# Seven quarter products for eight: Strassen's algorithm in the first half of an FFN behind attention

## The chip, the core and the metric

The kernel runs on one core of a Trainium2 chip. The metric is the device time of one execution in microseconds (us), the median of several runs. Beside it stands one execution recorded by the hardware profiler, with every instruction's start and length. The engines are TensorE (PE, matrix products; its weight loads are listed as PEld), VectorE (DVE), ScalarE (ACT), GpSimd (POOL) and SyncE (SP), which here issues all DMAs.

## The reference

Attention with normalized queries and keys, and then an FFN with two linear branches that are multiplied:

```python
# q, k, v: (8, 12, 448, 64); g_q, g_k: (64,)
q_n, k_n = rmsnorm(q, g_q), rmsnorm(k, g_k)       # x / sqrt(mean(x*x) + 1e-6) * g
attn = softmax(q_n @ k_n.T / 8)
x = (attn @ v).transpose(0, 2, 1, 3).reshape(3584, 768)
a, b = x @ w_a, x @ w_b                           # (768, 1536) each
out = (a * b) @ w_out                             # (1536, 768)
```

The weights arrive as float64; the kernel reads them as pairs of 32-bit words and rounds them to float32 itself. All products are in float32, and each float32 matmul is two instructions on TensorE.

## The kernel before

**Attention** is done by pairs of heads: 8 batches x 6 pairs are 48 pairs p. SP loads q, k and v; the squares are summed, POOL raises the means to the power -0.5 (L315), DVE scales q (L319), TensorE transposes k and q (L336), and ACT or DVE copy them into `qkT`. For each quarter c of the keys, TensorE makes the scores of both heads (L362), ACT the exponentials into `ET` (L368), and TensorE multiplies v by them into `o` (L381). The softmax's divisors come from `sums_over_keys`: a product with ones (L411) and a reciprocal on DVE (L415). For the first 12 pairs (`LEAD`) TensorE sums all four quarters of the keys; later DVE and POOL add them up first (L393, L395). `put_out` copies `o` (L460) and multiplies it by the reciprocal (L465) into `xT`, the transposed input of the FFN. A pair is written into its batch's block of tokens; blocks are cut at multiples of 128 tokens, so they hold 384 and 512 in turn, and what is over goes through `tail` into the next.

**The FFN** (`ffn(b)`, one block): for each of 12 column groups m and each of the weights a and b, 6 matmuls of 128 rows add up a bank `pf` (L491); ACT copies the bank of a into `hT` (L500) and DVE multiplies it by the bank of b (L502). Then for each 128 tokens and each half of the output 12 matmuls make `po` (L515); DVE or ACT copy it (L524, L526) and SP stores it. `pf` and `po` share two PSUM banks (tag `mm`); `hT` has one buffer, `xT` two.

**The weights** are made in 72 units of 384 columns (`weights(n)`): a DMA, one step on ACT (L250), five on DVE (L251 to L258), one on POOL (L260). The units of w_a and w_b, 48, come first, and use w_out's place for their raw words; then come w_out's 24.

**The order** is written by a planner, `Plan`. Every operation has an engine, an estimated length, a key, and the names that it reads and writes. The planner runs all of them in a model of the engines: each time it takes, on the engine that can start first, the ready operation with the lowest key (on TensorE among those that can start within 0.2 us of the first). Operations with the same `chain` stay together. The result is a fixed order for each engine's queue, which then runs in that order. The keys of attention are pair numbers, up to 48; those of the FFN start at 10,000. So TensorE does attention when some is ready, and FFN otherwise:

```python
op("PE", len(cs) * N / 600, key, products, ...)        # key = 1e4 + b * 1e3
op("PE", 0.76, p, product, ..., mode="rows", chain=chain)
```

## Time and profile before

| | |
|---|---|
| Median of 3 runs | 1820.95 us (1819.86 to 1821.93) |
| The profiled execution | 1819.57 us |
| Its span, first to last instruction | 1817.8 us |
| Mean granted TensorE clock | 0.991 |
| ACT busy | 384.3 us (21%) |
| POOL busy | 457.3 us (25%) |
| DMA | 73.43 MB, 40 GB/s over the span |

The page gives, for each engine, the busy time in us, its share of the span and the number of instructions. A line of a group names the source line, the engine, the operation, output<-input, the shape and the count; then come busy time, the mean of one in ns, the idle time of the engine just before these instructions, and what ended that. A line of the timeline gives the start, the length and what ran (merged with its like, xcount), and in brackets the idle time before it with what ended it. L numbers are lines of the kernel above. Lengths of matmuls include the filling and draining of the array, so consecutive ones overlap in the record; pitches from start to start do not.

### The profile page before, as it was taken

What the parts mean: (1) busy time and instruction counts of PE and PEld (TensorE: products, weight loads), DVE (VectorE), ACT (ScalarE), POOL (GpSimd) and SP (SyncE); (2) the same over time, 40 slices, a digit from 0 to 9 for tenths busy, and PEclk for the clock granted to TensorE, in tenths of its full rate; (3) what the DMA queues carried; (4) which work ended last, traced back from release to release, by engine and by line L of the source; (5) the groups of instructions that cost most, each with busy time, mean ns of one, the idle gap of its engine ahead of it and who ended that gap; (6) DMA issues with size and microseconds to landing.
All of it is one profiled execution on the core that took longest, in us unless ns stands there. A gap on an engine that the chain in (4) does not pass through costs nothing. (4 is left out here: it accounts for less than half of the span.)

```text
span 1817.8 us, 15323 instructions
## 1 busy us (share of the span) xinstructions
PE 1761.7 (97%) x5904; PEld 860.4 (47%) x5904; DVE 640.5 (35%) x872; ACT 384.3 (21%) x738; POOL 457.3 (25%) x276
## 2 busy tenths in 40 slices
PE   5899889999999999999999999999999999999998
PEld 2334444444444455544444455544444455554455
DVE  7999998640023410443004420245002420000000
ACT  5655323321013210232002320123101310000000
POOL 4444455550014420344004440145102210000000
PEclk8999999999999999999999999999999999999999
DMA  7444223110001100111001110011000100000000
GB/s 234 142 133 124 65 76 104 52 54 6 0 15 49 49 16 0 39 49 31 0 0 44 44 39 1 20 44 50 5 0 20 32 14 0 5 22 0 0 9 28
DMA packets 87317, 73.43 MB, mean 40 GB/s; under 512 B 49348, under 2 KB 78020, under 8 KB 87236
## 3 DMA queue, kind: packets, MB, share of 16 engines
q1 hardware_dynamic: 87236, 72.38, 14.1%
q8 instruction: 48, 0.79, 0.2%
q14 instruction: 33, 0.27, 0.1%
HBM read 61.34 MB, written 11.01 MB: 40 GB/s over the span
## 5 line engine op out<-in xcount | busy, mean ns | idle before, releaser
L491 PE MATMUL pf<-xT,w_b_sb 128*128 128x512 f32 (+1 forms) x1152 | 453.7, 543 | 9.8 <-DVE hT L502 9.8
L515 PE MATMUL po<-w_out_sb,hT 128*128 128x384 f32 x1344 | 453.1, 490 | 0.0
L491 PE MATMUL pf<-xT,w_a_sb 128*128 128x512 f32 (+1 forms) x1152 | 452.4, 541 | 0.0
L515 PEld LDWEIGHTS po<-w_out_sb,hT 128*128 128x128 f32 x1344 | 249.2, 190 | 193.2 <-issue 35.9
L491 PEld LDWEIGHTS pf<-xT,w_b_sb 128*128 128x128 f32 x1152 | 217.7, 191 | 229.2 <-issue 144.3
L491 PEld LDWEIGHTS pf<-xT,w_a_sb 128*128 128x128 f32 x1152 | 216.9, 190 | 215.8 <-issue 143.1
L502 DVE TENSOR_TENSOR hT<-hT,pf 128x384 f32<-128x384 f32 (+1 forms) x96 | 59.5, 620 | 700.3 <-PE pf L491 700.3
L368 ACT ACTIVATE ET<-sc,ms 112x448 f32<-112x448 f32 x384 | 212.4, 635 | 228.4 <-PE sc L362 227.3
L395 POOL TENSOR_TENSOR sum<-sum,ET 112x896 f32<-112x896 f32 x72 | 153.2, 2128 | 426.3 <-DVE sum L393 280.2
L415 DVE RECIPROCAL su<-su 128x448 f32<-128x448 f32 x48 | 142.3, 2964 | 147.3 <-PE su L411 147.3
L500 ACT COPY hT<-pf 128x384 f32<-128x384 f32 (+1 forms) x96 | 51.0, 532 | 662.3 <-PE pf L491 662.3
L381 PE MATMUL o<-ET,v_sb 112*64 112x448 f32 x768 | 175.1, 561 | 4.1 <-ACT ET L368 3.9
L362 PE MATMUL sc<-qkT 64*112 64x448 f32 x768 | 172.2, 568 | 4.9 <-DVE qkT L348 3.6
L315 POOL TENSOR_TENSOR ms<-ms,expo 112x16 f32<-112x16 f32 x48 | 141.8, 2953 | 26.7 <-DVE ms L311 25.1
L362 PEld LDWEIGHTS sc<-qkT 64*112 64x112 f32 x768 | 61.7, 174 | 111.6 <-issue 93.5
L381 PEld LDWEIGHTS o<-ET,v_sb 112*64 112x64 f32 x768 | 53.1, 138 | 104.5 <-issue 81.6
L302 DVE TENSOR_REDUCE ms<-sq 112x8 f32<-112x512 f32 x96 | 65.5, 682 | 84.1 <-POOL sq L296 76.8
L443 POOL COPY xT<-tail 128x384 f32<-128x384 f32 x4 | 2.0, 504 | 326.3 <-PE pf L491 323.1
L319 DVE TENSOR_TENSOR qn<-q_sb,ms 112x512 f32<-112x512 f32 x48 | 61.9, 1290 | 59.2 <-PE pt L336 47.3
L524 DVE COPY o_sb<-po 128x384 f32<-128x384 f32 x28 | 15.6, 557 | 144.6 <-PE po L515 144.6
L296 POOL TENSOR_TENSOR sq<-k_sb 112x512 f32<-112x512 f32 x36 | 38.0, 1056 | 71.5 <-DMA k_sb<-in_k_dram 70.2
L460 ACT COPY xT<-o 128x384 f32<-128x384 f32 (+1 forms) x48 | 24.2, 505 | 145.8 <-PE o L381 123.9
(54 smaller groups left out, 748.8 us busy)
## 6 DMA issues: line engine op xcount, KB each, us to landing
q_sb<-in_q_dram SPq DMA_DIRECT2D x48, 224.0 KB, 2.9
k_sb<-in_k_dram SPq DMA_DIRECT2D x96, 112.0 KB, 2.9
v_sb<-in_v_dram SPq DMA_DIRECT2D x48, 224.0 KB, 2.6
w_out_sb<-in_moe_w_a_dram SPq DMA_DIRECT2D x24, 384.0 KB, 3.8
w_out_sb<-in_moe_w_b_dram SPq DMA_DIRECT2D x24, 384.0 KB, 4.3
raw<-in_moe_w_out_dram SPq DMA_DIRECT2D x24, 384.0 KB, 3.1
out_dram<-o_sb SPq DMA_DIRECT2D x16, 168.0 KB, 2.1
out_dram<-o_sb SPq DMA_DIRECT2D x16, 144.0 KB, 2.0
```

Of the source, the lines that this page charges most:

```text
L302: nc.vector.tensor_reduce(rs[p][:, "qk".index(nm)], xs["sq", nm, p], AX, ALU.add)
L315: nc.gpsimd.tensor_tensor(msf, msf, expo, ALU.pow)
L319: nc.vector.tensor_tensor(qns[p].rearrange("p j h d -> p h j d"), xs["q", p].rearrange("p h (j d) -> p h j d", d=D), rs[p][:, 0].rearrange ...
L362: nc.tensor.matmul(t[:, e, 0:S], lhsT=qkTs[p][rows, 1, c * SP:(c + 1) * SP], rhs=qkTs[p][rows, 0, :], start=True, stop=True)
L368: nc.scalar.activation(E[:, e], scs[p, c][:, e, 0:S], AF.Exp, scale=rs[p][:, 1, 2 * c + e:2 * c + e + 1])
L381: nc.tensor.matmul(os_[p][e * D:(e + 1) * D, :], lhsT=xs["v", p][:, e, c * D:(c + 1) * D], rhs=ETs[p, c][:, e], start=(c == 0), stop=(c == ...
L395: nc.gpsimd.tensor_tensor(sums[p][0:SP], sums[p][0:SP], ETs[p, c], ALU.add)
L415: nc.vector.reciprocal(sus[p], sus[p])
L491: nc.tensor.matmul(pfs[m, n][:, 0:N], lhsT=w_sb[:, c, m * P:(m + 1) * P], rhs=xTs[b][:, c, 0:N], start=(c == 0), stop=(c == KA - 1))
L500: nc.scalar.copy(x, y)
L502: nc.vector.tensor_tensor(x, x, y, ALU.mult)
L515: nc.tensor.matmul(held["po"][:, 0:HALF], lhsT=hTs[0][:, m, t * P:(t + 1) * P], rhs=w_out_sb[:, m, h * HALF:(h + 1) * HALF], start=(m == 0 ...
```

## The change

The products x @ w_a and x @ w_b are made by Strassen's algorithm, one level deep (the variant with shared sums). An input block is two batches, 896 tokens: its quadrants are the two halves of the features (384 each) by the two batches (448 tokens each). There are four such blocks, beta = 0 to 3. The weights' quadrants are halves of the features by halves of the columns (768). Eight products of quarters become seven, of 3 matmuls of 448 columns each, with sums made beforehand and afterwards:

- *Inputs.* `put_out` writes quadrants `x{batch}.{half}` from a ring of 9 tiles. Four chained subtractions on DVE (`combine`, 1344 columns each) make T3, the new B12, T2 and T4. Every product of the block waits for T3 and T4. The blocks of 384 and 512 tokens and their tails are gone.
- *Weights.* For each of 12 rounds n = (m, ab), `factors(n)` loads four quadrants' pieces as float64 words in two parts (four DMAs, 1.57 MB), rounds them in steps of 768 columns, and makes three further factors with three DVE operations and one on POOL. The seven factors of a round, 1.376 MB, lie in a ring of three tiles (`st`); `keep` stores them in DRAM. Block 0 uses them as they are made; for blocks 1 to 3, `stream` loads them again (36 loads). Raw words of the first three rounds lie in `hT`'s place, those of the others in the last four rows of w_out's.
- *w_out.* Its 12 rows are rounded one at a time, 768 columns a step; rows 0 to 7 through a slot in `hT`'s place, rows 8 to 11 through `st` tiles once all the factors have begun.
- *Products.* A round runs a(B11), b(T2), a(B21), d(B12), g(T3), d(B22), g(T4); a, b, d and g are banks from the same ring of two as before. ACT, DVE and POOL put together the four quarters of a or of a*b from them in `hT`.
- *Attention.* In the first 12 pairs the transposes go through the `mm` banks, half a pair ahead, `qkT` has two buffers, the sums over the keys come in two parts of two quarters, and ACT copies them out of PSUM before the reciprocal. The reciprocal is made in two halves everywhere. Scores stand ahead of the previous pair's values in the chains.
- *Planner.* It models rings of tiles itself: an operation that opens a tile can't start before the tile's predecessor in the ring has had its last user. Its DMA rate goes from 200 to 250 bytes per ns.

The output products are as before, now over 7 tiles of 128 tokens a block. The core of the diff:

```diff
+            t, count = 0.0, {}
+            for x in members(n):
+                for name in ops[x][8]:
+                    tag, bufs = self.tags[name]
+                    had = opened.setdefault(tag, [])
+                    k = len(had) + count.get(tag, 0) - bufs
+                    count[tag] = count.get(tag, 0) + 1
+                    if k >= len(had):
+                        return None
+                    if k >= 0:
+                        if left[had[k]]:
+                            return None
+                        t = max(t, last[had[k]])
+            return t
...
-                    dma = max(dma, t) + ops[x][7] / 200.0
+                    dma = max(dma, t) + ops[x][7] / 250.0
...
+            for e, n, emit, r, wr in round_steps(get):
+                rate = {"ACT": 950, "DVE": 1900 if n == 1 else 950, "POOL": 420}[e]
+                op(e, 0.17 + size / rate, key, emit, [{"x": x, "w": w}[c] for c in r], [{"x": x, "w": w}[c] for c in wr])
...
+        def factors(n):
+            m, ab = order[n]
+            src = (moe_w_a, moe_w_b)[ab]
+            key = n * 1.1 + 0.5
+            st = tile_of(f"st{n}", "st", 3)
+            def begin():
+                sts[n] = ld.tile([P, 7, KH * P], FP32, tag="st", name="st", bufs=3)
+            op(None, 0.0, key, begin, [], [f"{st}/{x}" for x in range(7)] + ["streaming", "begun"], new=[st])
+            for part, quarters in enumerate((((0, 0), (0, 1)), ((1, 1), (1, 0)))):
+                if n < FIRST:
+                    at = 2 * n + part
+                    rows = [f"{hraw}/{at}"]
+                    words = lambda at=at: hold["h"][:, at * NW:(at + 1) * NW]
+                else:
+                    at = KO - 4 + 2 * part
+                    rows = [f"out{at}", f"out{at + 1}"]
+                    words = lambda at=at: w_out_sb[:, at:at + 2].rearrange("p a b -> p (a b)").bitcast(U32)
+                def load(words=words, quarters=quarters):
+                    for x, (i, j) in enumerate(quarters):
+                        nc.sync.dma_start(
+                            words()[:, 768 * x:768 * (x + 1)].rearrange("p (k n) -> p k n", k=KH),
+                            src[j * KH * P:(j + 1) * KH * P, 2 * (i * HM + m * P):2 * (i * HM + (m + 1) * P)].rearrange(
+                                "(k p) n -> p k n", p=P))
+                op("SP", 1.0, key - 2.5, load, [], rows, kb=768)
+                rounding(key, NW // 2, lambda words=words, part=part: (
+                    words().rearrange("p (n w) -> p n w", w=2), sts[n][:, 2 * part:2 * part + 2].rearrange("p a b -> p (a b)")),
+                    rows[0], f"{st}/{2 * part}")
+            parts = [0, 0, 2, 2, 4, 5, 6]
+            for e, us, to, x, y, alu in (("DVE", 0.6, 4, 3, 2, ALU.add), ("POOL", 1.05, 5, 0, 3, ALU.subtract),
+                                         ("DVE", 0.6, 3, 4, 0, ALU.subtract), ("DVE", 0.6, 6, 1, 3, ALU.subtract)):
+                op(e, us, key, lambda e=e, to=to, x=x, y=y, alu=alu: (nc.vector if e == "DVE" else nc.gpsimd).tensor_tensor(
+                    sts[n][:, to], sts[n][:, x], sts[n][:, y], alu),
+                   [f"{st}/{parts[x]}", f"{st}/{parts[y]}"], [f"{st}/{parts[to]}"])
...
+            def keep():
+                kept[n] = dram.tile([P, 7 * KH * P], FP32, name=f"kept{n}")
+                nc.sync.dma_start(kept[n], sts[n].rearrange("p a b -> p (a b)"))
+            op("SP", 0.5, key, keep, [f"{st}/{x}" for x in range(7)], [f"kept{n}"], kb=1376)
...
+        def stream(beta, n):
+            st = tile_of(f"st{beta}.{n}", "st", 3)
+            def load():
+                t = sts[beta, n] = ld.tile([P, 7, KH * P], FP32, tag="st", name="st", bufs=3)
+                nc.sync.dma_start(t.rearrange("p a b -> p (a b)"), kept[n])
+            op("SP", 0.5, 10.0 * beta + n / 2, load, [f"kept{n}"] + ([f"wl{kc}" for kc in range(KO)] if (beta, n) == (1, 0) else []), [f"{st}/{x}" for x in range(7)] + ["streaming"], new=[st], kb=1376)
...
+        def round_out(kc):
+            key, name = 11.5 + kc / 12, f"out{kc}"
+            raws = {}
+            if kc < WE:
+                st = f"{hraw}/{SLOTS - 1}"
             else:
-                st, name = f"out.{n % KO}", f"{'a' if dst is w_a_sb else 'b'}.{c}.{kc}"
+                st = tile_of(f"stout{kc}", "st", 3)
...
+                def move():
+                    x = wk.tile([P, 2, S], FP32, tag="sum", name="sum")[:, 0]
+                    nc.scalar.copy(x, sus[p])
+                    sus[p] = x
+                op("ACT", 0.55, p - 0.5, move, [su], [t, "moved"], new=[t])
+                su = t
+            for x in range(2):
+                half = slice(x * S // 2, (x + 1) * S // 2)
+                op("DVE", 1.55, p, lambda half=half: nc.vector.reciprocal(sus[p][:, half], sus[p][:, half]), [], [su])
...
+        def ffn(beta):
+            b = 2 * beta
+            B11, B21, B12, B22 = quad(b, 0), quad(b, 1), quad(b + 1, 0), quad(b + 1, 1)
+            key = 1e4 + beta * 1e3
...
+                op("DVE", 1.7, -0.5, emit, [x, y], [to], new=[to] if first else [])
+            T2, T3, T4 = (f"T{beta}.{n}" for n in (2, 3, 4))
+            combine(T3, B22, B12, True)
+            combine(B12, B12, B11, False)
+            combine(T2, B22, B12, True)
+            combine(T4, B21, T2, True)
...
+            for n, (m, ab) in enumerate(order):
+                if beta:
+                    stream(beta, n)
+                    st, at = f"st{beta}.{n}", (beta, n)
+                else:
+                    st, at = f"st{n}", n
+                quarter_products(beta, key, m, ab, st, at, (B11, B21, B12, B22, T2, T3, T4), h)
+            seven = 2 * S // P
+            for t in range(seven):
...
+            def product(bank, f, x, start, stop):
+                nm = f"p{ident_}.{bank}"
+                if start:
+                    tile_of(nm, "mm", 2)
...
+                def emit():
+                    if start:
+                        banks[bank] = ps_mm.tile([P, 512], FP32, tag="mm", name="pq")
+                    for c in range(KH):
+                        nc.tensor.matmul(banks[bank][:, 0:S], lhsT=sts[at][:, f, c * P:(c + 1) * P], rhs=quads[x][:, c],
+                                         start=(start and c == 0), stop=(stop and c == KH - 1),
+                                         skip_group_check=True)
+                op("PE", KH * S / 600, key, emit, [f"{st}/{(0, 0, 2, 2, 4, 5, 6)[f]}", x, T3, T4], [nm, "ffn"], new=[nm] if start else [], mode="full")
+                return nm
...
+            a = product("a", 0, B11, True, False)
+            if ab == 0:
+                take("ACT", 0.55, lambda: nc.scalar.copy(C(0, 0), PS("a")), [a], [hp[0]])
+            else:
+                t1 = tile("t1")
+                take("ACT", 0.55, lambda: nc.scalar.copy(fresh("t1", "t", 2), PS("a")), [a], [t1], [t1])
+            b_ = product("b", 3, T2, True, True)
+            if ab == 0:
+                take("DVE", 0.68, lambda: V.tensor_tensor(fresh("U", "U", 1), C(0, 0), PS("b"), ALU.add), [b_, hp[0]], [U], [U])
+            else:
+                take("DVE", 0.68, lambda: V.tensor_tensor(fresh("U", "U", 1), held["t1"], PS("b"), ALU.add), [b_, t1], [U], [U])
+            product("a", 1, B21, False, True)
+            if ab == 0:
+                take("ACT", 0.55, lambda: nc.scalar.copy(C(0, 0), PS("a")), [a], [hp[0]])
+            else:
+                take("DVE", 0.68, lambda: V.tensor_tensor(C(0, 0), C(0, 0), PS("a"), ALU.mult), [a], [hp[0]])
+            d = product("d", 4, B12, True, False)
+            if ab == 0:
+                take("DVE", 0.68, lambda: V.tensor_tensor(C(1, 1), held["U"], PS("d"), ALU.add), [d, U], [hp[1]])
+            else:
+                t2 = tile("t2")
+                take("DVE", 0.68, lambda: V.tensor_tensor(fresh("t2", "t", 2), held["U"], PS("d"), ALU.add), [d, U], [t2], [t2])
+            g = product("g", 5, T3, True, False)
+            if ab == 0:
+                take("DVE", 0.68, lambda: V.tensor_tensor(C(1, 1), C(1, 1), PS("g"), ALU.add), [g], [hp[1]])
+            else:
+                take("DVE", 0.68, lambda: V.tensor_tensor(held["t2"], held["t2"], PS("g"), ALU.add), [g], [t2])
+                take("POOL", 1.15, lambda: nc.gpsimd.tensor_tensor(C(1, 1), C(1, 1), held["t2"], ALU.mult), [t2], [hp[1]])
+            product("d", 6, B22, False, True)
+            product("g", 2, T4, False, True)
+            for bank, nm, i, n in (("d", "t3", 0, 1), ("g", "t4", 1, 0)):
+                if ab == 0:
+                    take("DVE", 0.68, lambda bank=bank, i=i, n=n: V.tensor_tensor(C(i, n), held["U"], PS(bank), ALU.add),
+                         [f"p{ident_}.{bank}", U], [hp[i]])
+                else:
+                    t = tile(nm)
+                    take("DVE", 0.68, lambda bank=bank, nm=nm: V.tensor_tensor(fresh(nm, "t", 2), held["U"], PS(bank), ALU.add),
+                         [f"p{ident_}.{bank}", U], [t], [t])
+                    take("POOL", 1.15, lambda i=i, n=n, nm=nm: nc.gpsimd.tensor_tensor(C(i, n), C(i, n), held[nm], ALU.mult),
+                         [t], [hp[i]])
...
-        for n in range(len(units)):
-            weights(n)
+        for n in range(len(order)):
+            factors(n)
+        for kc in range(KO):
+            round_out(kc)
```

`round_steps` gives the same steps as before: Abs on ACT; clamp, shift, sign, mask and the low part's scaling on DVE; the sum on POOL.

More of the change, by code (lines that the diff above doesn't have):

```diff
@@ new lines, in sums_over_keys @@
+            op("PE", 0.76 * len(cs) if p < LEAD else 0.76, p, spread,
+               [f"E{p}.{c}" for c in cs] if p < LEAD else [f"sum{p}"], [su], new=[su] if first else [], mode="cols", chain=chain)
+            if not last:
+                return
+            if p < LEAD:
+                t = tile_of(f"sum{p}", "sum", 1)
+                def move():
[4 more added lines that the diff above has]
+                su = t
```

444 lines of the change are left out of this document (230 added, 214 removed).

## The prediction

> **What bounds the kernel now.** I began with the page's totals, then took the chain of waits and TensorE's waits, then the timeline at places of each kind.
>
> ```profile
> span 1817.8 us, 15323 instructions
> ...
> PE 1761.7 (97%) x5904; PEld 860.4 (47%) x5904; DVE 640.5 (35%) x872; ACT 384.3 (21%) x738; POOL 457.3 (25%) x276
> ```
>
> TensorE (PE) is busy for all but 56.1 us. Busy time is modelled, so I price its work by pitch, from start to start, instead. The chain of waits ends in an undisturbed stretch of FFN; its columns are start, length and what:
>
> ```profile
> 1486.67 92.88 PE pf L491 x288
> ...
> 1625.99 123.60 PE pf L491 x288
> 1749.59 61.94 PE po L515 x192
> ...
> 1811.59 0.48 ACT o_sb L526
> ```
>
> Each line is one block of tokens: 288 instructions (two per matmul) of 384 columns in 92.88 us, of 512 columns in 123.60, and the output product at 0.3226 us per instruction. That is proportional to the columns within 1%, so a 448-column instruction should take (92.88 + 123.60) / 576 = 0.3758 us. Four blocks of each size make the first products 4 x 216.48 = 865.9 us; the output products, 1344 instructions, take 433.6.
>
> Attention beside FFN work, on the timeline (start, length, engine, line):
>
> ```profile
> 603.58 1.72 PE L381 MATMUL o<-ET,v_sb 112*64 112x448 f32 x8
> 605.23 1.76 PE L362 MATMUL sc<-qkT 64*112 64x448 f32 x8
> 606.92 4.14 PE L515 MATMUL po<-w_out_sb,hT 128*128 128x384 f32 x12
> ...
> 623.81 1.72 PE L381 MATMUL o<-ET,v_sb 112*64 112x448 f32 x8
> ```
>
> From 603.58 to 623.81 lies one head pair with three po groups of 12 (3 x 3.87): 20.23 - 11.61 = 8.6 us a pair. The first 12 pairs (p < LEAD) sum their keys on TensorE:
>
> ```profile
> 58.36 0.60 PE L336 MATMUL pt<-ident,k_sb 112*128 112x112 f32 x4 [0.51 <-ACT ET L368]
> ...
> 59.27 1.72 PE L381 MATMUL o<-ET,v_sb 112*64 112x448 f32 x8
> 60.83 3.18 PE L411 MATMUL su<-ET,ones 112*64 112x448 f32 x16
> ...
> 65.74 2.54 PE L381 MATMUL o<-ET,v_sb 112*64 112x448 f32 x8
> ...
> 70.48 0.60 PE L336 MATMUL pt<-ident,k_sb 112*128 112x112 f32 x4 [0.51 <-ACT ET L368]
> ```
>
> The pitch is 12.1 us, of which 0.51 is idle and 0.82 is an o group stretched by waiting for exponentials; 10.8 us is work. So 36 x 8.6 + 12 x 10.8 = 439 us of attention, and the work in all is 865.9 + 433.6 + 439 = 1739 us. TensorE ends at 1811.5, so 73 us are lost. The long idle times lie in the first 340 us, while the weights are rounded on VectorE (DVE):
>
> ```profile
> 0.00:25.00 25.00, 13.87 (x60) 5.88 (x62) 13.79 (x30) 14.63 (x28) 10.02 (x13) 1.00 0.82 263
> 200.00:225.00 25.00, 19.92 (x73) 10.44 (x71) 23.78 (x43) 6.59 (x14) 11.14 (x9) 1.00 0.35 97
> 250.00:275.00 25.00, 19.97 (x61) 10.30 (x61) 24.13 (x38) 2.98 (x6) 15.51 (x11) 0.93 0.30 81
> 400.00:1400.00 1000.00, 1000.00 (x3258) 485.32 (x3256) 256.19 (x294) 179.90 (x341) 235.89 (x130) 1.00 0.09 24
> ```
>
> The columns are stage, length, busy PE, weight loads, DVE, ACT, POOL, granted clock, DMA share, GB/s. Early, DVE is at 95%; from 400 us on TensorE never rests and DVE needs 26%. So the kernel is bound by TensorE's work, and what the change takes from that work counts in full, less the new holes that it leaves.
>
> **What it removes.** Per pair of batches there are 12 rounds (m, ab) of seven quarter products, each 3 matmuls of 448 columns: 42 instructions x 0.3758 = 15.8 us a round, 48 rounds, 757.6 us. That is 108.3 less than 865.9. Output products and attention keep their counts: 433.6 and 439. TensorE's work becomes 1630 us. The tails' copies go too; they were on ACT, DVE and POOL, off the path.
>
> **What it adds on other engines.** Drains of first products on DVE go from 96 to 264, on ACT from 96 to 72, and POOL gets 72 products.
>
> ```profile
> L502 DVE TENSOR_TENSOR hT<-hT,pf 128x512 f32<-128x512 f32 x48 | 33.0, 687 | 443.6 <-PE pf L491 443.6
> ...
> L415 DVE RECIPROCAL su<-su 128x448 f32<-128x448 f32 x48 | 142.3, 2964 | 147.3 <-PE su L411 147.3
> ```
>
> At 0.6 us for 448 columns (0.687 x 448/512) that is some 100 us more of DVE over the whole run, hidden beside TensorE while DVE is at 26%. The reciprocal, cut in two, blocks a drain for at most 1.5 us. The streams of kept factors are 36 loads of 1.376 MB: 5.2 us each at the 263 GB/s of the first window, against 15.8 us a round, with two spare buffers (31 us of cover). I cost them at nothing; with one buffer they would show by some 8 us a round. Such a load waits on SP for its buffer, and behind it on that queue stand q, k, v loads and the output stores; the stores' two buffers cover that for one 7.7 us output tile each.
>
> **The holes.**
>
> (a) The start. The first factor's words (key -2.0, first in the program) are issued ahead of q and k of pair 0, which have the same key.
>
> ```profile
> 4.93 0.98 PE L336 MATMUL pt<-ident,k_sb 112*128 112x112 f32 x4 [4.93 <-DMA k_sb<-in_k_dram]
> ...
> 12.61 3.30 PE L362 MATMUL sc<-qkT 64*112 64x448 f32 x8 [1.28 <-ACT qkT L346]
> ```
>
> 1.57 MB at 263 GB/s are 6.0 us, so the first scores start at 18.6 and not 12.6: 18.6 us lost before attention runs (bounds 12.6, if the queues share, and 21).
>
> (b) The lead. No FFN work fits between the first 12 pairs, since all products wait for the four quadrants. TensorE must live on attention alone, at between 10.8 us a pair (its work) and 12.1 (measured in such a stretch). A second qkT buffer and sums cut in two close part of the gap; DVE still rounds 28 of the 72 old units beside it. I take 11.8: 12 us lost (0 to 16).
>
> (c) Before the first product come the last divide and four chained DVE subtractions of 1344 columns, by L502's rate 1.8 us each: with the reciprocal some 11 us, half of it filled by pairs 12 and 13: 5 us (0 to 11).
>
> (d) The bubble. The mm ring has two banks: bank d opens only when a is drained, and a's drain starts when its second product ends. Nothing else of the FFN can go between. The nearest row is the copy after the last matmul, 0.48 us at 384 columns, starting 0.06 after TensorE's end (1749.59 + 61.94 = 1811.53). With 0.53 to 0.6 for 448 columns, a hand-over on each side of 0.1, and the 0.16 us by which back-to-back groups overlap (the o group at 59.27 is recorded to 60.99, the su group starts at 60.83), a hole is 0.95 us. There are 48; beside attention some are filled, about 8 in the 36 rounds that have any. 40 x 0.95 = 38 us (ends: 20 and 60). The other six hand-overs of a round have a product of 2.26 us beside a drain of 0.6.
>
> (e) Factors 3 to 11. Each is made while the products before it run, in a ring of three.
>
> ```profile
> L251 DVE TENSOR_SCALAR w_a_sb<-w_a_sb 128x384 f32<-128x384 f32 x24 | 8.8, 369 | 0.6 <-ACT w_a_sb L250 0.6
> ...
> L252 DVE TENSOR_SCALAR w_a_sb<-w_a_sb 128x384 uint32<-128x384 uint32 x24 | 26.3, 1096 | 0.8
> ...
> L254 DVE SCALAR_TENSOR_TENSOR w_a_sb<-w_out_sb,w_a_sb 128x384 uint32<-128x384 uint32 x24 | 14.8, 616 | 0.8
> ...
> L256 DVE TENSOR_SCALAR w_out_sb<-w_a_sb 128x384 uint32<-128x384 uint32 x24 | 9.3, 389 | 0.7
> ...
> L258 DVE SCALAR_TENSOR_TENSOR w_out_sb<-w_out_sb 128x384 f32<-128x384 uint32 x48 | 29.6, 617 | 1.3
> ```
>
> A 384-column unit costs DVE 3.09 us, a factor four of them, 12.4, and three additions of 384 columns (0.5 each): 14 us. With the 26% that the rest needs a factor takes 14 / 0.74 = 19 us of DVE. TensorE's side of a round in this stage, with 6 pairs shared out over 12 rounds, is 15.8 + 0.95 + 4.3 = 21 us. They are close; I take 6 us of stall (0 to 40). L252 is the row to note: the same shape as L251, yet 1.10 us against 0.37, in a stretch where POOL works on the same weights. The Trainium skill, "SBUF — State Buffer", section "Who interferes with whom", has a rule against the change here: a DVE instruction with two SBUF inputs and a GpSimd instruction that reads SBUF lock each other out for a whole instruction; by it the new additions and subtractions would each wait out a POOL product. The trace agrees for L252; the sum above stays as it is, since it uses the mean with such waits in it.
>
> (f) The last four rows of w_out are rounded after the last factors, and the output product waits for them; attention and the first halves of two tiles (7.7 us) cover most: 4 us (0 to 15).
>
> (g) Turns and slowed matmuls: 73 lost now, less 49.8 idle before TensorE's end, leaves 23; the early, slowed part shrinks: 10.
>
> Sum: 18.6 + 12 + 5 + 38 + 6 + 4 + 10 = 94; TensorE ends at 1630 + 94 = 1724. The last drain and store take 6.3 (1817.8 - 1811.5): span 1730. The profiled execution took 1819.57, 1.8 over its span, and the median of the runs is 1.4 above that: 1733 us, 4.8% below 1820.95.
>
> **The rivals.**
>
> The bubbles fill. The plan puts an attention group into a hole when one is ready, and the lead runs at 10.8: 18 + 12 us less, and no stall in (e): about 1700. Against it: the last 12 rounds have no attention beside them, and a pair offers only three such groups.
>
> The clock drops. The window at 250 us shows holes of over 2 us with a granted clock of 0.93, the one at 200 us like holes with 1.00. If a hole in every round held 0.93 through the products, 757.6 x (1/0.93 - 1) = 57 us more: 1790. The Trainium skill, "TensorE: Matmul & The Clock Gate", section "A second HAM failure mode: psum-queue depth-cycling", says that small idle times between groups, from cycling through PSUM banks, can make the gate oscillate. The trace speaks against it for holes under 1 us: even those over 2 us left 1.00 in one window of two.
>
> The factors set the pace. If load, rounding and additions of one factor run one after another instead of overlapping, a factor takes c us and the stage 3 x 16.8 + 9c against TensorE's 12 x 16.8 + 52; it decides from c = 22.5 on. At c = 27 it costs 40 us (1773). It ends slower than before from c = 33: at 34, 1733 + 9 x 11.5 = 1837. For it: the words have two slots, so a load waits for the rounding of the one before. Against it: DVE has room for 19.
>
> The saving isn't there, because 448-column matmuls of short groups of three run slower than the interpolation, say at the pace of 512: 757.6 x 512/448 = 866: 1841. The proportional rows speak against it.
>
> **How the numbers follow.** Forecast 0.73; bubbles fill 0.11; clock 0.04; factors mildly 0.06, to beyond the old time 0.04; no saving 0.02. What a measurement can tell from no change is 0.2%, 3.6 us. The first four are faster: 0.94, from which I move 0.01 to the band round no change, which lies between the two cases of the factors. The range takes in the forecast with its terms' ends (start, lead and bubble 30 lower; 40 higher by the factors) and half of the filled bubbles: 1703 to 1773.
>
> **What would show it.** In the changed profile: 2016 instructions of first products at 0.376 us pitch; first scores near 18.6; the first product near 170; a hole of about 0.95 us once a round, released by ACT or DVE after the drain of bank a, each time in the last 12 rounds; granted clock 1.00 after 300 us; DVE near 750 us busy. I'd be wrong if holes at other banks appear (DVE late with a drain), if TensorE waits for a factor's tile for more than 40 us in all, or if the lead takes far more than 12 us a pair.

## The result and the profile after

The changed kernel takes 1731.86 us (median of 4 runs, 1731.24 to 1732.12), the kernel before 1821.44 on the same chip (1819.86 to 1822.2): a ratio of 0.951, 95% interval 0.949 to 0.953. The forecast was 1733. The page of the kernel after begins:

```profile
span 1730.2 us, 14844 instructions
...
PE 1650.3 (95%) x5616; PEld 803.3 (46%) x5616; DVE 742.7 (43%) x936; ACT 372.2 (22%) x666; POOL 543.1 (31%) x320
```

There are 288 TensorE instructions fewer, as the plan says (5904 - 5616), and the span is 87.6 us shorter. The timeline of TensorE, after (start, length, engine, line, operation, count; in brackets the idle time ahead and what ended it):

```profile
19.07 3.33 PE L483 MATMUL sc<-qkT 64*112 64x448 f32 x8 [0.73 <-ACT qkT L468]
...
52.73 0.63 PE L461 MATMUL pt<-ident,qn 112*128 112x112 f32 x2 [8.91 <-DVE qn L432]
...
82.59 0.60 PE L461 MATMUL pt<-ident,k_sb 112*128 112x112 f32 x4
...
93.21 0.60 PE L461 MATMUL pt<-ident,k_sb 112*128 112x112 f32 x4
...
173.12 2.43 PE L657 MATMUL pq<-x,st 128*128 128x448 f32 x6
...
178.87 4.82 PE L657 MATMUL pq<-x,st 128*128 128x448 f32 x6 [3.31 <-DVE x L592]
189.35 3.33 PE L483 MATMUL sc<-qkT 64*112 64x448 f32 x8 [5.67 <-DVE qkT L470]
...
481.27 3.33 PE L483 MATMUL sc<-qkT 64*112 64x448 f32 x8 [12.29 <-DVE qkT L470]
...
1424.09 189.58 PE L657 MATMUL pq<-x,st 128*128 128x448 f32 x504
```

Read it from the end. The last 12 rounds are one line: 504 instructions in 189.58 us, 0.376 us each, and not one hole. Where the prediction had a bubble in each of these rounds there is none. The longest holes lie early, and behind the start each waits for VectorE: for a normalized q (L432), for the four chained sums (L592), for the scaled copy of q's transposes (L470). In the plan every product waits for those sums; in the trace the first one, B11's at 173.12, ran ahead of them, and the second, which reads T2, waited. TensorE's waits, summed over the run (us in total, times, longest):

```profile
PE sc L483 <- DVE qkT L470: 30.9, 13, 12.3
PE pt L461 <- DVE qn L432: 17.3, 3, 8.9
PE pt L461 <- DMA k_sb<-in_k_dram: 9.8, 1, 9.8
PE pq L657 <- DVE U L685: 3.4, 2, 1.7
```

To see where the time went I price TensorE's instructions of each stretch by their undisturbed pitch (L657 0.3758 us, L625 0.3226, scores 0.211, o 0.205, su 0.2, transposes 0.10) and subtract that from the stretch. The whole work comes to 757.6 + 433.6 + 425.1 = 1616.3 us; TensorE ends at 1722, so some 105 us are lost (the prediction: 1630 and 94). Kernels of the experiments are beside it; an instruction on a boundary counts on both sides, some 2 us in all.

| Stretch, us | after | e1 strict banks | e2 w_out last | e5 unrounded | e6 sums on DVE | e12 also copies on ACT |
|---|---|---|---|---|---|---|
| 0 to 100 | 37.1 | 37.1 | 37.5 | 37.5 | 37.1 | 42.5 |
| 100 to 173.1 | 0.8 | 0.5 | 2.5 | 0.7 | 0.8 | 0.0 |
| 173.1 to 202.9 | 14.6 | 13.8 | 9.2 | 4.1 | 11.9 | 3.4 |
| 202.9 to 350 | 15.7 | 18.7 | 19.0 | 4.0 | 15.2 | 14.0 |
| 350 to 500 | 19.7 | 29.3 | 13.6 | 3.5 | 10.5 | 12.6 |

From 500 us to the end of TensorE's work the kernel after loses 15.3 us, of which 0.1 after 1424.

Not all of a loss is waiting. Where the granted clock is lower, matmuls take longer: the six instructions at 173.12 take 2.43 us, the six at 178.87, in a window with a granted clock of 0.66 (shown with e5), take 4.82. The table counts this as lost too.

### The profile page after: what moved, and what is told of

Same layout as the page of the kernel before. It is cut to its first block, busy times and chain, and to the rows that moved or that the text cites. A ratio compares the mean times of both kernels' runs of the same rounds, so it can differ in the third digit from the quotient of the medians.

```text
span 1730.2 us, 14844 instructions
## 1 busy us (share of the span) xinstructions
PE 1650.3 (95%) x5616; PEld 803.3 (46%) x5616; DVE 742.7 (43%) x936; ACT 372.2 (22%) x666; POOL 543.1 (31%) x320
## 5 line engine op out<-in xcount | busy, mean ns | idle before, releaser
L657 PE MATMUL pq<-x,st 128*128 128x448 f32 x2016 | 772.5, 542 | 12.3 <-DVE U L685 3.4
L657 PEld LDWEIGHTS pq<-x,st 128*128 128x128 f32 x2016 | 379.6, 190 | 395.4 <-issue 372.1
L625 PE MATMUL po<-w_out_sb,hT 128*128 128x384 f32 x1344 | 443.5, 488 | 0.0
L625 PEld LDWEIGHTS po<-w_out_sb,hT 128*128 128x128 f32 x1344 | 251.8, 190 | 182.7 <-issue 15.9
L483 PE MATMUL sc<-qkT 64*112 64x448 f32 x768 | 176.9, 581 | 32.3 <-DVE qkT L470 30.9
L557 DVE RECIPROCAL su<-su 128x224 f32<-128x224 f32 x72 | 112.7, 1565 | 165.1 <-PE su L539 164.1
L704 POOL TENSOR_TENSOR hT<-hT,t 128x448 f32<-128x448 f32 x24 | 27.2, 1132 | 475.6 <-DVE t L703 475.6
L428 POOL TENSOR_TENSOR ms<-ms,expo 112x16 f32<-112x16 f32 x48 | 142.8, 2974 | 54.2 <-DVE ms L424 42.9
L637 ACT COPY o_sb<-po 128x384 f32<-128x384 f32 x28 | 13.4, 479 | 273.3 <-PE po L625 258.0
L715 POOL TENSOR_TENSOR hT<-hT,t 128x448 f32<-128x448 f32 x48 | 55.5, 1159 | 40.6 <-DVE t L713 40.6
L679 ACT COPY hT<-pq 128x448 f32<-128x448 f32 x24 | 12.8, 532 | 254.8 <-PE pq L657 254.8
L709 DVE TENSOR_TENSOR hT<-U,pq 128x448 f32<-128x448 f32 x48 | 29.8, 620 | 71.3 <-PE pq L657 71.3
L682 ACT COPY t<-pq 128x448 f32<-128x448 f32 x24 | 12.8, 532 | 210.1 <-PE pq L657 210.1
L267 POOL TENSOR_TENSOR st<-st,w_out_sb 128x768 f32<-128x768 f32 x18 | 34.0, 1887 | 68.5 <-DVE w_out_sb L265 49.7
L432 DVE TENSOR_TENSOR qn<-q_sb,ms 112x512 f32<-112x512 f32 x48 | 53.5, 1114 | 4.0 <-POOL ms L428 3.2
```

Of the source, the lines that this page charges most:

```text
L267: ("POOL", 2, step(lambda hi, hif, lo, lof, w, wb: nc.gpsimd.tensor_tensor(w, w, lof, ALU.add)), "x", "w"))
L428: nc.gpsimd.tensor_tensor(msf, msf, expo, ALU.pow)
L432: nc.vector.tensor_tensor(qns[p].rearrange("p j h d -> p h j d"), xs["q", p].rearrange("p h (j d) -> p h j d", d=D), rs[p][:, 0].rearrange ...
L483: nc.tensor.matmul(t[:, e, 0:S], lhsT=qkTs[p][rows, 1, c * SP:(c + 1) * SP], rhs=qkTs[p][rows, 0, :], start=True, stop=True)
L557: op("DVE", 1.55, p, lambda half=half: nc.vector.reciprocal(sus[p][:, half], sus[p][:, half]), [], [su])
L625: nc.tensor.matmul(held["po"][:, 0:HALF], lhsT=hTs[0][:, m].rearrange("p a s -> p (a s)")[:, t * P:(t + 1) * P], rhs=w_out_sb[:, m, x * HA ...
```

## The experiments

The theories: that the saving is there in full, and that the losses left are VectorE's, which is full or works in the wrong order until the first block's factors are rounded. Against it: that the predicted bubble is there and something else is cheaper than thought; that the early holes are plain matters of order, each to be closed by itself; that one buffer or another holds the stages up. The letters of the theories are explained in the expectations. Every edit is planned anew, so it can also change the order of work that it does not name. All times are medians; the kernel before took 1819.8 to 1820.5 beside these runs.

**e1: the banks strictly in turn.** One tag for each of the two banks, so that each tile takes the bank that is not the last one's:

```diff
+            turns[0] += 1
+            return ps_mm.tile([P, 512], FP32, tag=f"mm{turns[0] % 2}", name=name, bufs=1)
...
-                        banks[bank] = ps_mm.tile([P, 512], FP32, tag="mm", name="pq")
+                        banks[bank] = next_bank("pq")
```

The same for pt and po.

> The two banks of the products are handed out strictly in turn (a, b, a's bank for d, b's bank for g), where the changed kernel's instructions let d wait for b's drain and g for a's. Theory A: the hole after the second a product, 0.95 us a round, is real whenever d must take a's bank, and the changed kernel escapes it only because d gets the bank that was drained a product earlier. Then the last 12 rounds go from 189.6 us to 199 to 201, and the whole from 1731.9 to 1768 to 1777 us (40 to 48 holes). Theory B: the hand-over is hidden by TensorE's queue whatever the bank; the last 12 rounds stay at 189.6 and the whole at 1732.

Measured: 1775.24 us, ratio 0.975 (0.973 to 0.977), 43.4 us more than after. The timeline of TensorE in the last rounds, and TensorE's waits:

```profile
1463.32 16.05 PE L663 MATMUL pq<-x,st 128*128 128x448 f32 x42 [0.62 <-ACT hT L696]
...
1480.09 16.05 PE L663 MATMUL pq<-x,st 128*128 128x448 f32 x42 [0.71 <-DVE hT L698]
```

```profile
PE pq L663 <- DVE hT L698: 27.4, 24, 2.7
...
PE pq L663 <- ACT hT L696: 17.4, 22, 2.5
```

From one hole to the next it is now 16.7 us in the mean, in place of 15.8: the bubble of (d) in the size that was forecast (0.95), once a round, with the drain of a as its releaser. In the kernel after, the same drain runs beside TensorE; the timeline of all engines there:

```profile
1461.67 35.87 PE L657 MATMUL pq<-x,st 128*128 128x448 f32 x95
...
1462.62 0.53 ACT L690 COPY hT<-pq 128x448 f32<-128x448 f32 x1 [3.98 <-PE pq L657]
```

In 46 of the 48 rounds of the kernel after, the first matmul of d starts before the drain of a has begun, in all 48 after VectorE's reading of b (U); the first matmul of g starts after the drain of a in all 48. So the ring gives product d the bank that came free first. That is b's: it was drained while a's second product ran. g then gets a's bank, whose drain has run beside d's three matmuls.

**e2: the rounding of w_out's rows behind everything else.**

```diff
-            rounding(key, DM, lambda: (raws[1].rearrange("p (n w) -> p n w", w=2), w_out_sb[:, kc]), st, name)
+            rounding(key + 50, DM, lambda: (raws[1].rearrange("p (n w) -> p n w", w=2), w_out_sb[:, kc]), st, name)
```

> Only the keys of the rounding steps of w_out's rows go up by 50, behind all of attention. Theory A: the holes of 5.7 us near 184 and 12.3 us near 469, both ended by DVE's copy of q into qkT, come from the order, because DVE's queue has whole rounding chains ahead of that copy; both go, 10 to 16 us less: 1716 to 1722. Theory C: DVE simply has too much to do in that stage; the order only moves the wait to the output product, which needs the rows: 1730 to 1740.

Measured: 1726.67 us, ratio 0.948 (0.946 to 0.949), 5.2 us less than after. TensorE's waits:

```profile
PE sc L483 <- DVE qkT L470: 17.6, 11, 3.7
```

The 12.3 us hole is gone, but half of the gain came back: the stretch from 203 to 350 us loses 19.0 in place of 15.7. What is put off in one place has to be done in another on the same engine.

**e3: pair 0's q and k ahead of the first factor's words.**

```diff
-                op("SP", 1.0, key - 2.5, load, [], rows, kb=768)
+                op("SP", 1.0, key - (2.0 if n == 0 else 2.5), load, [], rows, kb=768)
```

> Only the loads of the first factor's words are put behind q, k, the gains and v of the first pair. Theory A: the first scores go from 19.1 to 12.6 us and the end by 4 to 6 us: 1726 to 1728. Theory C: the lead is bound by DVE's rounding of the first factors, so the hole of 8.9 us at the fourth pair grows by what the start gains: 1731 to 1733.

Measured: 1745.33 us, ratio 0.959 (0.957 to 0.960), 13.5 us more: both expectations missed. The first scores do come at 12.0 us and not 19.1, and nothing of it reaches the first product (174.8 us against 173.1). The timeline of TensorE, then the windows (busy PE, weight loads, DVE, ACT, POOL, granted clock, DMA share, GB/s):

```profile
30.64 1.01 PE L461 MATMUL pt<-ident,qn 112*128 112x112 f32 x4 [8.87 <-DVE qn L432]
...
208.65 3.69 PE L657 MATMUL pq<-x,st 128*128 128x448 f32 x5 [8.47 <-ACT hT L679]
```

```profile
25.00:50.00 25.00, 17.86 (x78) 6.94 (x80) 24.72 (x24) 12.86 (x22) 13.44 (x7) 0.75 0.69 233
50.00:75.00 25.00, 18.56 (x88) 7.02 (x86) 24.57 (x31) 13.76 (x26) 13.81 (x6) 0.86 0.36 115
```

VectorE is busy for 49.3 of these 50 us: the lead that starts earlier meets the same rounding, and waits. The second hole is a new one: the first drain writes hT, whose place still holds raw words of w_out's row 7, since loading and rounding them were pushed back.

**e8: e3, and the words of w_out's rows 0 to 7 spread over the seven slots** (e3's edit, and):

```diff
-                st = f"{hraw}/{SLOTS - 1}"
+                slot = (SLOTS - 1, 0, 1, 2, 3, 4, 5, SLOTS - 1)[kc]
+                st = f"{hraw}/{slot}"
```

> As e3_qk_first, and w_out's rows 0 to 7 take their raw words in the seven slots in hT's place in turn, not all through the last one. Theory G: the first block's hT can't open before the last of these rows is rounded, and one slot makes load and rounding of the rows a chain that ends after the lead; with it gone, the earlier start counts and the hole at the first drain goes: first product near 168, 1716 to 1723. Theory C: DVE is full in the lead: 1731 or more.

Measured: 1745.05 us, ratio 0.959 (0.957 to 0.960). The hole at the first drain is gone, which agrees with the slot as its cause, as in e3 the first drain waited for the last step of a row of w_out (POOL L267, 7.3 us); but the rows that now load early are rounded in the lead, and there TensorE's timeline has a longer one:

```profile
69.11 1.01 PE L462 MATMUL pt<-ident,qn 112*128 112x112 f32 x4 [13.84 <-DVE qn L433]
```

The first product moves to 197.9 us. Work put off the end of the lead costs as much in its middle.

**e4: the eighth product.** The product of B22 is made twice, so that a round has eight products; the sums of its bank are changed by it.

```diff
+            product("d", 6, B22, False, False)
             product("d", 6, B22, False, True)
```

> Each round runs its product d(B22) twice, so that there are eight products again (the sum is changed by it). Theory A: TensorE is the bound in every round, and a product costs its 6 x 0.3758 = 2.256 us in full: 48 x 2.256 = 108.3 more, 1838 to 1842. Theory C: DVE paces the first 12 rounds, so an added product there fills holes: 10 to 20 us less than that, 1820 to 1830.

Measured: 1827.46 us, ratio 1.004 (1.003 to 1.005), 95.6 us more than after for 288 instructions of 0.3758 us (108.2). The 12.6 us that don't show were free: from 350 to 500 us the loss falls from 19.7 to 3.4, where more work of TensorE's own now stands. So a product less is worth nearly its full price, and what is missing from it is missing before 500 us.

**e5: factors 3 to 11 unrounded.** Of their rounding only the first step (Abs) is left; the others are left out.

```diff
-            for e, n, emit, r, wr in round_steps(get):
+            for e, n, emit, r, wr in round_steps(get)[:1 if 3.5 < key and size == NW // 2 else 7]:
```

> Factors 3 to 11 keep only the first rounding step (Abs on ACT); five steps on DVE and one on POOL are left out for each of their 18 parts, so these factors lose their signs and low bits. Theory C: the 21 us lost between 203 and 465 us come from DVE being late with drains and copies because it rounds factors there; the loss falls to some 10: 1718 to 1723. Theory D: they come from turns between attention and products and from attention's own chain, and stay: 1728 to 1732.

Measured: 1694.81 us, ratio 0.931 (0.930 to 0.933), 37 us less than after, more than twice what was expected. The windows, of after and then of e5:

```profile
175.00:200.00 25.00, 16.02 (x40) 5.67 (x40) 17.14 (x17) 5.54 (x10) 14.07 (x7) 0.66 0.12 35
200.00:350.00 150.00, 139.37 (x486) 60.53 (x483) 122.95 (x149) 43.18 (x75) 87.51 (x52) 1.00 0.38 125
350.00:500.00 150.00, 135.04 (x411) 64.01 (x411) 105.33 (x134) 29.25 (x47) 63.66 (x39) 0.95 0.38 131
```

```profile
175.00:200.00 25.00, 21.12 (x79) 9.04 (x79) 18.18 (x20) 6.54 (x12) 13.47 (x7) 1.00 0.16 39
200.00:350.00 150.00, 147.12 (x505) 67.67 (x506) 78.05 (x103) 46.33 (x78) 71.78 (x45) 1.00 0.43 147
350.00:500.00 150.00, 147.12 (x507) 71.65 (x506) 62.13 (x81) 36.07 (x62) 52.89 (x33) 1.00 0.35 120
```

From 200 to 350 us VectorE falls from 82% busy to 52%, and the losses from 173 to 500 us fall from 50.0 to 11.6. So the making of the factors costs some 37 us there, though no wait of TensorE's names a factor: its waits name the normalization and the copies, which stand behind the rounding in VectorE's queue. The 37 us hold more than VectorE's time: GpSimd's last step of the rounding is left out too, and the granted clock, 0.66 from 175 to 200 us and 0.95 from 350 to 500 us in the kernel after, is 1.00 in e5. How much belongs to each is not separated.

**e6: the partial sums of the exponentials on VectorE, not GpSimd.** 72 instructions from pair 12 on.

```diff
-                    nc.gpsimd.tensor_tensor(sums[p], sums[p], ETs[p, c], ALU.add)
+                    nc.vector.tensor_tensor(sums[p], sums[p], ETs[p, c], ALU.add)
...
-                op("POOL", 2.1, p, emit, [f"E{p}.{c}"], [t])
+                op("DVE", 1.12, p, emit, [f"E{p}.{c}"], [t])
```

> From the 13th pair on the sums over the keys' last two quarters are made on DVE and not on POOL (72 operations; 2.2 us each on POOL, 1.08 for this shape on DVE). Theory E: POOL and DVE lock each other out, so DVE's rounding steps of 0.56 and 0.96 us, now 1.0 to 1.4 in the mean, come down beside it, and DVE's busy time rises by less than the 78 us that it takes over: 1724 to 1732. Theory C: DVE's load is what counts; 20 us more of it in the first block make holes: 1736 to 1745.

Measured: 1713.13 us, ratio 0.941 (0.940 to 0.943), 18.7 us less than after, better than any expectation: the engine that the kernel waits for got 72 instructions more, and the kernel became faster. One thing that happens shows at the first drain. The timeline after, of VectorE, and of GpSimd at the same time:

```profile
181.82 2.31 DVE L260 TENSOR_SCALAR w_out_sb<-w_out_sb 128x768 uint32<-128x768 uint32 x1
184.16 2.71 DVE L262 SCALAR_TENSOR_TENSOR w_out_sb<-hraw,w_out_sb 128x768 uint32<-128x768 uint32 x1
```

```profile
181.46 4.60 POOL L519 TENSOR_TENSOR sum<-sum,ET 112x896 f32<-112x896 f32 x2 [8.71 <-DVE sum L517]
```

And VectorE's timeline of e6 there:

```profile
181.07 2.29 DVE L519 TENSOR_TENSOR sum<-sum,ET 112x896 f32<-112x896 f32 x2
...
183.86 0.56 DVE L260 TENSOR_SCALAR w_out_sb<-w_out_sb 128x768 uint32<-128x768 uint32 x1
184.45 0.96 DVE L262 SCALAR_TENSOR_TENSOR w_out_sb<-hraw,w_out_sb 128x768 uint32<-128x768 uint32 x1
```

Two sums on GpSimd take 4.60 us and stretch the two instructions of VectorE that start beside them from 0.56 and 0.96 to 2.31 and 2.71; on VectorE the two sums take 2.29 and nothing is stretched. The 3.5 us of stretching are more than the 2.29 us of work. The Trainium skill, "SBUF — State Buffer", section "Who interferes with whom", says that the port pair which VectorE and GpSimd share is an exclusive lock, held for a whole instruction while the other blocks, and names instructions with two SBUF inputs and tensor_scalar in its two-port modes as those that need it; both rows agree. Over the run the group of L432, after and then in e6 (busy, mean ns of one, idle ahead), shows the same:

```profile
L432 DVE TENSOR_TENSOR qn<-q_sb,ms 112x512 f32<-112x512 f32 x48 | 53.5, 1114 | 4.0 <-POOL ms L428 3.2 <-PE pt L461 0.8
```

```profile
L432 DVE TENSOR_TENSOR qn<-q_sb,ms 112x512 f32<-112x512 f32 x48 | 38.4, 800 | 8.2 <-POOL ms L428 7.3 <-PE pt L461 0.9
```

VectorE got 80.6 us of sums (72 x 1.119), but its busy time rose only from 742.7 to 800.3: 23 us of stretched time went, 15 of them at L432 alone. So over the run VectorE has more to do, not less, and what counts is where the time goes.

After 500 us the loss falls by some 7 us, and there the trace shows the stretching as the cause. VectorE is busy for only 35% of the time from 500 to 1400 us. The timeline of the kernel after:

```profile
862.93 4.57 POOL L519 TENSOR_TENSOR sum<-sum,ET 112x896 f32<-112x896 f32 x2 [26.06 <-DVE sum L517]
...
863.21 2.35 DVE L432 TENSOR_TENSOR qn<-q_sb,ms 112x512 f32<-112x512 f32 x1
...
865.48 0.67 DVE L470 TENSOR_SCALAR qkT<-pt,gain 128x448 f32<-128x448 f32 x1
...
866.20 1.76 PE L483 MATMUL sc<-qkT 64*112 64x448 f32 x8 [1.44 <-DVE qkT L470]
```

A normalization of 0.69 us takes 2.35 beside the sums, the copy behind it is late, and the scores wait for 1.44 us. From 500 us on TensorE waits for a copy on VectorE five times, 7.2 us in all, each time behind a normalization stretched like this one; in e6 it is 0.5 us.

Before 500 us less is settled. From 173 to 203 us the loss falls by 2.7 us; from 203 to 350 us, where VectorE is fullest, next to nothing is gained. From 350 to 500 us it falls by 9.2 us, as the 12.3 us hole goes; but there the order is another too: in e6 the rounding of the two rows of w_out starts at 461.6 us, in the kernel after at 467.5, right ahead of the copy. How much of the 9.2 us is stretching, of which 3.5 us stand in that hole, and how much is order was not tested. That GpSimd's shorter queue helps by itself is not borne out at L432, whose idle time for GpSimd (L428) rose from 3.2 to 7.3 us, but no run excludes it.

**e7: one qkT buffer.** `"qkT", 2` becomes `"qkT", 1`, in the plan and in the tile.

> qkT has one buffer again. Theory A: the lead's pitch of 10.6 us a pair comes from the second buffer, with one it is 11.5 to 12.1 as before: 10 to 16 us more, 1742 to 1748. Theory F: the split sums alone carry it: 1731 to 1735.

Measured: 1733.79 us, ratio 0.952 (0.951 to 0.954), 1.9 us more than after: within the spread. The second buffer, to which (b) gave part of the lead's better pitch, carries at most 2 us.

**e9: a later key for the rounding of factors 0 to 2.**

```diff
+            late = key + 10 if n < FIRST else key
...
-                rounding(key, NW // 2, lambda words=words, part=part: (
+                rounding(late, NW // 2, lambda words=words, part=part: (
```

The factors' additions and stores get the same key.

> The change is as in the kernel after; only the order in which VectorE and GpSimd take the work is other: the rounding of factors 0 to 2 gets a later key, so that it stands behind the normalizations of the lead instead of ahead of the one of pair 3. Theory C (VectorE is full from the lead to the end of the first block; a hole closed in one place comes back in another): the hole of 8.9 us at 52.7 us goes, the first product is earlier by 5 to 9 us, but the rounding then meets the first block's work and the holes after the first drain grow; 1724 to 1734, that is -8 to +2 us. Rival H (the hole is a plain loss of the order, the first block has room): all 8.9 us are gained, 1721 to 1724. Rival I (the first product needs factor 0 and waits for it): slower, 1735 to 1745.

Measured: 1734.97 us, ratio 0.953 (0.951 to 0.954), beside 0.949 to 0.953 of after. It did not do what it was for. TensorE's waits:

```profile
PE pt L462 <- DVE qn L433: 18.9, 3, 10.3
```

The hole stands at 10.3 us, and the rounding of a row still stands ahead of that normalization on VectorE. So it says nothing on the theories: with other work due later, what was ready took its place, and the key alone doesn't order the lead.

**e10 and e11: the edits together.** e10 is e2 and e6; e11 is e10 and e9.

> Both edits that gained alone: the 72 partial sums of the exponentials on VectorE instead of GpSimd, and the rounding of the rows of w_out that the last part of the set-up needs behind the first block's other work. Alone they were worth 18.7 and 5.2 us. If they take away different holes (the first one the doubled durations beside GpSimd, the second the queue order at 481 us) the sum is 1707 to 1709. If both gain by the same thing, the time that VectorE has left at the first drain, it is 1711 to 1714.

> The last kernel and the later rounding of factors 0 to 2 together. Theory C with room made on VectorE by taking GpSimd's sums off the shared time: 1700 to 1708. If the factors' rounding behind the lead takes the room again: 1708 to 1716.

Measured: 1714.85 us (ratio 0.941, 0.940 to 0.943) and 1716.16 us (0.943, 0.941 to 0.945). Neither is faster than e6 alone. In e6 the longest wait of the scores for VectorE's copy is 5.2 us already, not 12.3, so that there is little left in putting the rows off. e10's losses lie in other places: 10.4 us from 203 to 350 us (15.2 in e6), but 19.2 from 350 to 500 us (10.5 in e6), where a long wait is back. TensorE's waits in e10:

```profile
PE sc L483 <- DVE qkT L470: 16.7, 7, 8.6
```

So the two gains don't add; that both came from the same time on VectorE fits the total, but the trace shows holes that moved.

**e12: e6, and q's scaled copies on ScalarE in every pair**, as in the lead.

```diff
-                    elif p < LEAD:
-                        nc.scalar.activation(qkTs[p][:, 0], pts[p, 0][:, 0:S], AF.Copy, scale=gain[:, 0:1])
                     else:
-                        nc.vector.tensor_scalar_mul(qkTs[p][:, 0], pts[p, 0][:, 0:S], gain[:, 0:1])
+                        nc.scalar.activation(qkTs[p][:, 0], pts[p, 0][:, 0:S], AF.Copy, scale=gain[:, 0:1])
```

> The kernel e6 (the 72 partial sums on VectorE) with the scaled copies of q's transposes on ScalarE from pair 12 on, as they are in the lead; 36 copies of 0.676 us leave VectorE, 24.3 us in the whole run, and the scores wait in ScalarE's queue, which is busy 28% from 203 to 350 us. Theory C (VectorE is what the first block waits for, by its load and by its queue): the waits of the scores for VectorE's copy, 12.2 us in e6, become under 4 us, and the time falls from 1713 to 1701 to 1709. Rival K (the waits only change their name, since the normalization ahead of the transposes stays on VectorE, and the exponentials wait behind the copy on ScalarE): 1710 to 1718.

Measured: 1706.63 us (1706.04 to 1709.33), ratio 0.938 (0.936 to 0.939): 6.5 us less than e6, 25 less than after, the fastest kernel here that computes the whole. TensorE's waits:

```profile
PE pt L461 <- DVE qn L432: 21.7, 5, 11.9
PE pt L461 <- DMA k_sb<-in_k_dram: 11.4, 1, 11.4
PE sc L481 <- ACT qkT L468: 6.3, 4, 2.5
PE po L623 <- POOL w_out_sb L267: 4.8, 1, 4.8
```

The waits of the scores for a copy, 30.9 us after and 12.2 in e6, are 6.3 now, and at ScalarE. What stands first in the list is the lead, which no experiment made shorter.

## Why the prediction was right, and where it was wrong

The total was right by 1 us because errors met: a bubble of 38 us that isn't there and 14 us of attention's work too much stand against some 48 us by which the other losses were sized too small. That the sum came out is luck; that the saving is there in full is not.

- **TensorE's work** (1630). The bound, the pitch (0.3758, measured 0.376) and the count of 2016 held, and e4 shows that an eighth product in every round is worth its price up to 13 us in all. Attention comes to 425.1 us, not 439: the 14 us are part of the luck. The rival without a saving is out.
- **(a) The start** (18.6). First scores at 19.1: right. That the 6.5 us could be won back by the order of the loads was not claimed, and e3's order did not win them back, with VectorE full in the lead.
- **(b) The lead** (12). The undisturbed pitch is 10.6 us, near the bound by work; but from the first scores to the first product some 20 us are lost (37.1 + 0.8, less the 18.3 ahead of the scores, which is 19.1 less eight transposes), 8.9 of them in one hole. A mean pitch was the wrong form for it. What makes the hole is not settled: e9 did not move it.
- **(c) to (f) without the bubble: the last sums, the factors, w_out's rows** (5 + 6 + 4 = 15). From 173 to 500 us 50.0 are lost. This is the second step that failed, and in it the size of (e): the prediction divided a factor's VectorE time by the share that was free and compared it with a round, which asks whether a factor is late. Factors are not late. They delay, in VectorE's queue, the small instructions for which the scores wait. e5 puts their price at 37 us, the lower clock included (bounds given: 0 to 40). (f) is mixed with it: the holes of 5.7 and 12.3 us stand behind the rounding of w_out's rows, and e2 closes the longer one by moving that alone, but no wait of the kernel after names a row. Two ways by which VectorE's time reaches TensorE show in e6 and e12: instructions stretched beside GpSimd's sums, and copies late in the queue. The prediction named the lock of the two engines and gave it no term of its own. It read L252 as agreeing with the rule of two SBUF inputs; that row has one input (`w_a_sb<-w_a_sb`) and can't show it. The stretched rows with two are L262 and L432.
- **(d) The bubble** (38). This is the step that failed: "bank d opens only when a is drained". Its size was right, 0.94 us a round in e1, but in the kernel after d takes the bank of b, which is free by then. Strict turns cost 43.4 us of 48 x 0.94 = 45, so that attention hardly fills them, as the prediction held against its rival. Holes at other banks, a sign of being wrong by its own words, come to 8.3 us in all (3.4 for U, 4.9 for other drains).
- **(g) Turns and slowed matmuls** (10). 15.3 us from 500 us on, and 0.1 of them in the rounds with nothing beside them: slightly low. About half of them are the waits that e6 took away.
- **The rivals.** The holes that "the bubbles fill" wanted away are indeed absent, but by the choice of bank and not by attention; its 1700 us needed a quiet first block too, and with two edits that take waits away e12 comes to 1707. The factors did set a price, not a pace. The clock stayed at 1.00 after 500 us, as the forecast had it; it fell to 0.66 from 175 to 200 us, where the holes are 3.3 and 5.7 us long, and for matmuls slowed there the prediction had only a part of the 10 us of (g).

## What to carry to other kernels

Before a price is put on a hand-over between buffers, list the order in which they come free: a ring that gives out the first free one can hide a drain that strict turns would show, and here it was worth 43 us. When an engine off the path is nearly full in a stretch (here 82%), don't ask only whether its big job is in time, but which small instructions queue behind it and who waits for them; three of the four edits that only reordered such work gained nothing or lost, while moving GpSimd's sums gained 19 us and taking the copies off VectorE 6. Count as an engine's time also what another engine's instructions add to its own: moving work onto the busier engine can make the kernel faster.

## What the runs showed of the hardware

A GpSimd sum of 896 columns takes 2.2 us (mean of 72, beside other work), the same on VectorE 1.12, and a VectorE instruction that starts beside it can take longer by as much as it runs on (0.56 us becomes 2.31, 0.96 becomes 2.71, 0.69 becomes 2.35). At single places, such as the first drain, this costs more than the sums would on VectorE (3.5 us against 2.29); over the run it is 23 us against 80.6.

A hole of 0.6 to 0.7 us in every round, 16.7 us apart, did not lower the clock in e1's last rounds. The window of e1 (columns as above):

```profile
1500.00:1600.00 100.00, 95.99 (x253) 47.26 (x252) 20.24 (x33) 4.79 (x9) 10.17 (x9) 1.00 0.22 83
```

The Trainium skill, "TensorE: Matmul & The Clock Gate", section "A second HAM failure mode: psum-queue depth-cycling", tells of a kernel whose short idle times between groups made the clock oscillate; with fp32 products and one hole in 42 instructions the granted clock here stays at 1.00, so for holes of this length the measurement speaks against its holding in this case.

Longer holes in the same kernel went with a lower clock. From 350 to 450 us e1 has holes of 2.5 and 2.6 us, the granted clock is 0.97, and the 42 instructions behind one of them take 17.75 us where others take 16.05. TensorE's timeline of e1, then the window:

```profile
381.11 17.75 PE L663 MATMUL pq<-x,st 128*128 128x448 f32 x42 [2.51 <-DVE hT L698]
```

```profile
350.00:400.00 50.00, 45.98 (x120) 21.61 (x119) 36.90 (x47) 9.64 (x15) 22.03 (x15) 0.97 0.34 123
```
